# Two whole experts before the router, six after it; two attention units in flight; a new static order of steps

## The chip, the cores and the metric

The kernel runs on one core of a Trainium2 chip. The metric is the device time of the program in microseconds (us). The engines of the core are named as in the profile: PE (TensorE, the matrix engine; PEld is its weight load), DVE (VectorE), ACT (ScalarE), POOL (GpSimd) and SP (SyncE), which only issues DMAs here.

## What is computed

Attention with a decaying state, per batch (4) and head (8), over 768 tokens with a head size of 48; its output is read as 3072 tokens of 384 numbers, and a mixture of 8 experts follows. Every expert sees every token; the router only weighs the experts' outputs, and its weights need all tokens at once (the sums over axis 0).

```
state = alpha[t][:, None] * state + k[t] (x) v[t];   y[t] = q[t] @ state
x = y as [3072, 384]
P = exp(x @ w_gate - max);  8 times: P /= P.sum(1); P /= P.sum(0); P *= N / E
out = sum over e of P[:, e:e+1] * (relu(x @ w1[e]) @ w2[e])      # 384 -> 1024 -> 384
```

## The kernel before

**Two phases.** As the router's weights are known only when the last token is through the attention, the kernel computes whole experts early, beside the attention: for experts 0 to NA-1 (NA = 3) it stores the unweighted output of every token in DRAM (`raw`, evac_raw L275). The other experts come late, after the router (`sinkhorn` L998), and add weighted into `accd`. All matmuls of the experts are made of 16-bit halves, three passes each (PASSES).

**Early expert work** is cut into units of 256 tokens of one expert (moe_tile L236). A unit has 16 pieces: 8 of the first layer (9 matmuls of 256 columns each, tile `ps`, then ACT and DVE write the two halves of `h`) and 8 of the second (6 matmuls of 384 columns; after every fourth ACT copies the sum to `r`, which goes to `raw`). The list `waiting` (L910) opens a unit when its tokens and weights are there. `load_expert` (L157) loads and splits the weights of an early expert.

**Late expert work** goes by a scheme with seven products where eight blocks stand (first L1205, second L1407): per tile of 256 tokens 66 matmuls of 256 columns (`p1a`, `p1c`, `p1d`) and 84 of 192 (`p2x`, `p2y`, `p2v`). `load_late` (L1042) loads, splits and combines the weights of a late expert; for the first one, with w3_, that is done in the transition, beside the last early units, and for the others beside the expert ahead. The first two tiles of the first late expert have no partner yet: `first_one` (L1298) computes them in sixteen steps, and the loop at L1348 puts those between the last early pieces.

**Attention** goes by chunks of 128 tokens, 24 in all. The first four (direct_chunk L339) are computed from the inputs alone, in many small steps on PE and DVE. For the others a block of 256 tokens (attn_block L478, "b" steps) first works in a layout of 16 tokens per row: products on POOL (`tmp`), sums on DVE (`AB`), decays on both (`qt`, `kt`, `al`). There are ten such blocks, numbers 2 to 11. The block's results go to DRAM (`qs`, `ks`, `As`, `ds`) and come back in another layout (`QN`, `KN`, `an`, `DN`). Then attn_decays ("d") and, for each chunk, attn_chunk and attn_tail ("c", six steps): transposes into `Tk` and `Tq`, decayed copies (`deck`, `decq`), score matmuls (`psl`), the score tile `A` (POOL spreads `an` over it with `mask`), output (`psy`), state (`ST`), and at the end the chunk's router scores (`lg`, written by DVE from `psg`). All blocks use one set of buffers. turn_x (L770, "t") makes the combinations of x that the late experts need, on POOL.

**The order** of all steps of the early phase is the string ORDER (L40): b, w (weights), c, d, t, v (first weights of the late expert) and g (router weights) with the number of their block, expert or chunk; a capital letter moves a few operations from POOL to DVE or ACT. "f" is early expert work for 0.45 us of a time account (fill, L870). A step that may not run yet is put off (early_ L949, run L972). The engines then take their instructions in that program order, each engine in order, and wait for each other by semaphores. All DMAs are issued by SP, in order too.

## Time and profile before

| | |
|---|---|
| time, median of 3 runs | 1631.6 us (1631.49 to 1633.08) |
| the profiled execution, first to last instruction | 1630.9 us |
| PE busy | 1589.6 us (97%) |
| DVE busy | 1272.1 us (78%) |
| ACT busy | 932.6 us (57%) |
| POOL busy | 391.8 us (24%), all of it before 720 us |
| DMA | 188.5 MB, 39.8% of 16 engines |

How to read it: the profile is one execution. A busy share is an average over very different stages, so the table by stage, below, is the one to use. PE's spans are modelled, so that a busy PE need not do useful columns all the time. The chain of waits leads back from the last instruction to what released it at each step. A stage's idle time counts only on the engine that the others wait for.

The stages of the profiled execution: start (to 163 us, when the first chunk from a block has its scores), attention beside early experts (163 to 720), transition (720 to 797: the router's loop, the last early units and the first late steps) and the late experts (797 to 1625).

### The profile page before, as it was taken

The page shows a single profiled execution, that of the slowest core. Times are in us where ns is not written, and L with a number is a line of the kernel's source. Part 1 is how long each engine was busy: PE and PEld are TensorE (multiplying, and loading weights), DVE is VectorE, ACT ScalarE, POOL GpSimd, SP SyncE. Part 2 cuts the span into 40 slices and gives each one's busy share as a digit, 9 for nine tenths or more (in the row PEclk, how much of TensorE's full clock was granted, in tenths as well). Part 3 has the DMA queues.
Part 4 walks back from the last instruction along what each step waited for, and adds up shares of the span by engine and source line. Part 5 has one row for each costly group of instructions (what it writes and reads, how often), then busy time and mean ns, then how long its engine had stood idle before and what let it go on. Part 6 is the DMA issues. An engine that isn't in the chain of part 4 may idle for free.

```text
span 1630.9 us, 45380 instructions
## 1 busy us (share of the span) xinstructions
PE 1589.6 (97%) x18855; PEld 1370.0 (84%) x18855; DVE 1272.1 (78%) x2845; ACT 932.6 (57%) x2249; POOL 391.8 (24%) x402
## 2 busy tenths in 40 slices
PE   7799999999999999999999999999999999999999
PEld 5676777777777777777899999999999999999998
DVE  7978576755767655357879988998799879989997
ACT  4557443343343433435688877766776677665554
POOL 4526556845756743310000000000000000000000
PEclk9899999999999999999999999999999999999999
DMA  9262445154156143240433362326333532335443
GB/s 186 59 151 75 105 101 117 52 128 102 43 124 141 56 107 74 76 168 26 120 119 130 115 187 95 121 95 194 101 100 122 172 130 95 131 106 168 157 148 127
DMA packets 194654, 188.51 MB, mean 116 GB/s; under 512 B 115088, under 2 KB 175248, under 8 KB 194448
## 3 DMA queue, kind: packets, MB, share of 16 engines
q1 hardware_dynamic: 194448, 185.62, 39.8%
q8 instruction: 147, 2.41, 0.6%
q14 instruction: 59, 0.48, 0.1%
HBM read 129.76 MB, written 55.82 MB: 114 GB/s over the span
## 4 chain that ended last, share of the span: by engine, by line
PE 81%; DVE 11%; ACT 3%; issue 2%; DMA 1%; POOL 1%; SPq 0%; DVEq 0%; ACTq 0%; POOLq 0%
PE ps L66 30%; PE p1a L66 14%; PE p2x L66 12%; PE p2y L66 6%; PE p1c L66 4%; PE p1d L66 3%; PE p2v L66 3%; PE psl L66 2%; DVE h L57 2%; PE psy L66 2%; DVE hf L57 1%; DVE w L57 1%; DVE acc L57 1%; DVE AB L57 1%; PE pskn L69 1%
## 5 line engine op out<-in xcount | busy, mean ns | idle before, releaser
L66 PEld LDWEIGHTS <-h 128*128 128x128 f16 x6768 | 593.6, 98 | 119.8 <-issue 10.1
L66 PEld LDWEIGHTS <-w 128*128 128x128 f16 x4896 | 463.8, 98 | 64.3 <-issue 13.3
L57 DVE TENSOR_TENSOR h<-hf,h 128x256 f16<-128x256 f32 x480 | 286.3, 616 | 31.5 <-ACT h L57 31.0
L66 PE MATMUL ps<-xT,w 128*128 128x256 f16 (+1 forms) x2664 | 300.2, 270 | 4.1 <-DVE h L57 2.7
L66 PE MATMUL ps<-w,h 128*128 128x384 f16 x1728 | 298.5, 329 | 4.0 <-DVE w L57 2.9
L66 PE MATMUL p1a<-x,w 128*128 128x256 f16 (+1 forms) x1860 | 289.2, 269 | 4.4 <-ACT v L57 2.2
L66 PE MATMUL p2x<-w,h 128*128 128x192 f16 x2832 | 272.1, 246 | 0.0
L57 ACT CAST h<-hf 128x256 f16<-128x256 f32 x480 | 250.7, 571 | 14.8 <-DVE hf L57 10.8
L57 DVE TENSOR_TENSOR hf<-hf 128x256 f32<-128x256 f32 x480 | 182.1, 420 | 29.4 <-ACT hf L57 24.5
L66 PE MATMUL p1a<-x,wx 128*128 128x256 f16 (+1 forms) x744 | 199.6, 269 | 1.0 <-DVE p1c L57 1.0
L57 DVE SCALAR_TENSOR_TENSOR h<-ps,h 128x256 f16<-128x256 f32 (+1 forms) x296 | 115.7, 411 | 101.9 <-ACT h L57 100.7
L57 POOL TENSOR_TENSOR tmp<-qt,kt 128x768 f32<-128x768 f32 (+2 forms) x86 | 149.1, 1740 | 144.0 <-DMA kt<-in_k_dram 76.2
L57 ACT ACTIVATE h<-ps 128x256 f16<-128x256 f32 (+1 forms) x296 | 109.3, 376 | 129.7 <-PE ps L66 127.8
L66 PEld LDWEIGHTS <-wx 128*128 128x128 f16 x1736 | 167.3, 98 | 17.3
L57 ACT ACTIVATE hf<-p1d 128x256 f32<-128x256 f32 x120 | 46.0, 383 | 166.7 <-DVE h L57 140.9
L66 PE MATMUL p2y<-w,h 128*128 128x192 f16 x1416 | 136.1, 246 | 0.0
L57 ACT COPY r<-ps 128x384 f32<-128x384 f32 x72 | 34.3, 478 | 146.3 <-PE ps L66 112.5
L57 DVE TENSOR_REDUCE AB<-tmp 128x16 f32<-128x768 f32 (+2 forms) x90 | 81.1, 902 | 45.2 <-POOL tmp L57 44.3
L66 PE MATMUL p1c<-x,wx 128*128 128x256 f16 (+1 forms) x372 | 98.8, 269 | 0.0
L66 PE MATMUL p1d<-x,wx 128*128 128x256 f16 (+1 forms) x620 | 85.2, 269 | 0.0
L57 ACT COPY A<-psl 16x128 f32<-16x128 f32 (+3 forms) x148 | 49.2, 335 | 40.6 <-PE psl L66 39.1
L57 ACT ACTIVATE hf<-p1c 128x512 f32<-128x512 f32 x120 | 70.9, 591 | 0.0
(233 smaller groups left out, 1939.0 us busy)
## 6 DMA issues: line engine op xcount, KB each, us to landing
x<-xd SPq DMA_DIRECT2D x60, 704.0 KB, 5.4
accd<-acc SPq DMA_DIRECT2D x48, 384.0 KB, 3.2
acc<-accd SPq DMA_DIRECT2D x48, 384.0 KB, 3.2
raw<-r SPq DMA_DIRECT2D x72, 192.0 KB, 1.9
ri<-raw SPq DMA_DIRECT2D x72, 192.0 KB, 3.8
xT<-in_moe_w_dram SPq DMA_DIRECT2D x8, 768.0 KB, 5.5
w1f<-in_moe_w_dram SPq DMA_DIRECT2D x16, 384.0 KB, 7.4
w2f<-in_moe_w_dram SPq DMA_DIRECT2D x8, 768.0 KB, 6.6
```

Of the source, the lines that this page charges most:

```text
L57: r = f(*a, **k_)
L66: tc.keep_in_program_order(nc.tensor.matmul(out_, lhsT, rhs, start=start, stop=stop, **k_))
L69: tc.keep_in_program_order(nc.tensor.transpose(out=out_, in_=in_, identity=idn))
```

## The change

- NA goes from 3 to 2: experts 0 and 1 are early, 2 to 7 late. (A number TC allows the second early expert to take only the first tokens; it is set to all 3072.) The late list LATE has six experts. The raw outputs to be added are one with the first late expert and one with the last, where it was one and two.
- Blocks are computed on two sets of buffers in turn (`apx`, beside `ap1`), so that two are under way at once, except for blocks 2 and 3.
- A block's scores go to DRAM as 64 by 64 squares with zeros in place (`AS`, cleared twice by the new "z" steps), and come back with two DMAs per chunk straight into `A`. The POOL operation that made `A` out of `an` and `mask` is gone, and so are `an`, `mask`, and the clearing of `A` for each direct chunk. `ds` and `DN` are gone too: two matmuls with the identity give the decays (`psd`), and DVE copies them (`DT`), a 17th block step. `v` comes with one DMA per chunk where it was two.
- ORDER is new. "f" now is exactly one piece (piece). Conditions in early_ follow the new buffers.
- In the transition, w3_ starts only when one expert is left among the early units (before: when no unit of expert 0 was left), two turn steps move into the router's loop, and the first late tile gets eight steps between the last early pieces; the second tile's eight come after them. Tiles of late weights are renamed `lw`.

```diff
-    ORDER = 'D2 c6 C0 f f f f f f f f f f C0 f ...
-    NA = 3
+    ORDER = 'C0 C0 g C0 C0 B2 b2 b2 C0 B2 c1 w0 W0 g C0 B2 ...
+    NA = 2
+    TC = 3072
...
+    AA = [ap1.tile([P, H, P], F32, name=f"A{i}") for i in range(2)]
+    for x in AA:
+        GE.memset(x, 0.0)
+    AS = [dr.tile([H, NCH, P // BK, BK * BK + BK], F32, tag=f"As{i}", bufs=1, name=f"As{i}") for i in range(2)]
+
+    def clear_scores():
+        for x in AS:
+            SP.dma_start(x.rearrange("h c i a -> (h c i a)").rearrange("(p n t) -> p n t", n=5, t=208),
+                         AB[1].rearrange("p s t -> p (s t)")[:, :208].unsqueeze(1).to_broadcast([P, 5, 208]))
+            yield
...
     def load_v(x, b, t0):
-        for r in range(2):
-            SP.dma_start(x[:, :, r * DP:r * DP + D], v[b].rearrange("(j r) t d -> r t j d", r=2)[r, t0:t0 + P])
+        SP.dma_start(x.rearrange("p j (r e) -> p (j r) e", r=2)[:, :, :D], v[b, :, t0:t0 + P].rearrange("h t d -> t h d"))
...
-        qt, kt, al = (ap1.tile([P, 16, D], F32, tag=x, name=f"{x}_{nm}") for x in ("qt", "kt", "al"))
+        home = twin[0] if g > ND // NCH + 1 and g % 2 == 0 else ap1
+        qt, kt, al = (home.tile([P, 16, D], F32, tag=x, name=f"{x}_{nm}") for x in ("qt", "kt", "al"))
...
-        put(0, U)
-        dma(ds.rearrange("h n d -> n h d"), al[:, 0])
-        if True:
-            dma(As.rearrange("h (n s) t -> n h (s t)", s=16), Af)
+        psd = psa.tile([P, 512], F32, tag="psa", name=f"psd_{nm}")
+        for r in range(2):
+            mm(psd[r * DP:r * DP + D, :P], al[:, 0], ident)
+        for x, y in ((ks, ko), (qs, qo)):
+            dma(x.rearrange("h (n t) d -> (h n) (t d)", t=16), y.rearrange("p t d -> p (t d)"))
+        As_ = As[0]
+        dma(bass.AP(tensor=As_.tensor, offset=As_.offset, ap=[[16 * BK + 16, P], [BK, 16], [1, 16]]), A)
...
-        A = ap2.tile([P, H, P], F32, tag="A", name=f"A_{nm}")
-        GE.tensor_mul(A.rearrange("p h (n t) -> p n h t", t=16),
-                             got["an"][:, c].unsqueeze(1).to_broadcast([P, 8, H, 16]),
-                             mask.unsqueeze(2).unsqueeze(3).to_broadcast([P, 8, H, 16]))
+        A = AA[tt % 2]
+        for i in range(P // BK):
+            tok = slice(i * BK, (i + 1) * BK)
+            SP.dma_start(A[tok, :, tok], got["As"][:, c, i, :BK * BK].rearrange("h (s t) -> s h t", s=BK))
...
+    def piece():
+        if filler and (filler[0][2] != FT or filler[0][0] in ready):
+            x = filler[0]
+            next(x[1])
+            x[2] += 1
+            if x[2] == FT + 4 * (x[4] // P):
+                filler.pop(0)
...
-            while any(x[0] == 0 for x in filler):
-                yield 9.0
...
-    todo = [(e, t0) for e in range(NA, E) for t0 in range(0, NT, G)]
+    todo = [(e, t0) for e in LATE for t0 in range(start(e), NT, G)]
...
-        if n > 3:
+        if n == 2 or n == 3:
+            turn()
+        if n > 3 and len({x[0] for x in filler}) < 2:
             some(w3_, 0.45)
...
-            n = next(lead, None)
+            n = next(lead, None) if not filler or len(led) < 8 else None
...
-    RAWS = {NA: (0,), E - 1: (1, 2)}
+    RAWS = lambda e, t0: (0,) if e == NA else (NA - 1,) if e == E - 1 and t0 < TC else ()
```

How the change moves instructions is shown at three places. First, DVE around the score write of chunk 4, the first chunk that comes from a block (`lg` with `psg_0_4`). `h1` rows are evacuations of early first-layer pieces, `w21` rows weights of the last early expert. Before:

```order
L57 SCALAR_TENSOR_TENSOR w21_2_2265<-xT0_2_84,s_w2_2_2495,w20_2_2264 128x768 x2
L57 COPY p2t_89<-psg_0_4_2547 128x1
L57 TENSOR_SCALAR lg_88<-psg_0_4_2547,p2t_89,ipwg_93 128x8
L57 TENSOR_TENSOR Tq_0_5_2463<-Tq_0_5_2463,q128_0_2_1844 128x512
L57 SCALAR_TENSOR_TENSOR h1_2_0_2626<-ps1_2_0_0_2627,h0_2_0_2625 128x256
```

And now:

```order
L58 SCALAR_TENSOR_TENSOR h1_1_0_2213<-ps1_1_0_5_2320,h0_1_0_2212 128x256
L58 COPY p2t_85<-psg_0_4_2332 128x1
L58 TENSOR_SCALAR lg_84<-psg_0_4_2332,p2t_85,ipwg_89 128x8
L58 SCALAR_TENSOR_TENSOR w21_1_2131<-xT1_2_83,s_w2_1_2210,w20_1_2130 128x768
L58 TENSOR_SCALAR wsc_86<-p_w1_1_1474,p_w2_1_2207 128x1
```

Ahead of that write, PE has 216 first-layer matmuls of 256 columns, 144 of 128 and 192 of the second layer before, and 126, 144 and 96 now. On DVE 40 evacuations and 17 weight operations stand ahead of it before, 30 and 12 now.

Second, POOL at a chunk's decayed copy (`deck64`), in batch 2. Before:

```order
L57 TENSOR_TENSOR tmp1_2_2_55_6416<-qt_2_2_6107,kt_2_2_6108 128x384
L57 TENSOR_TENSOR deck64_2_2_6438<-Tk_2_2_6423,suf_1_137 128x256
L57 TENSOR_TENSOR A_2_2_6440<-an_2_1_6091,mask_71 128x8x8x16
L57 TENSOR_TENSOR kt_2_2_6108<-kt_2_2_6108,al_2_2_6109 128x8x48
L57 TENSOR_TENSOR tmp2_2_2_56_6459<-qt_2_2_6107,kt_2_2_6108 128x384
```

And now:

```order
L58 TENSOR_TENSOR tmp4_2_1_52_4669<-qt_2_1_3693,kt_2_1_3694 128x768
L58 TENSOR_TENSOR deck64_2_0_4710<-Tk_2_0_4695,suf_0_133 128x256
L58 TENSOR_TENSOR tmp4_2_2_53_4740<-qt_2_2_4662,kt_2_2_4663 128x768
L58 TENSOR_TENSOR tmp4_2_1_54_4742<-qt_2_1_3693,kt_2_1_3694 128x768
L58 TENSOR_TENSOR Tk_2_0_4695<-Tk_2_0_4695,k128_2_0_4646 128x512
```

The operation on `A` is gone, and products of two blocks (2_1 and 2_2) alternate where those of one block stood.

Third, DVE in the transition, at the second tile of the first late expert (`p1d_3_256` before, `p1d_2_256` now; `hf`, `h` and `p1c` belong to it too). Before:

```order
L57 SCALAR_TENSOR_TENSOR h1_2_2816_11673<-ps1_2_2816_7_11903,h0_2_2816_11672 128x256
L57 TENSOR_TENSOR xT1_0_85<-xT1_0_85,xT0_0_82 128x2x192
L57 TENSOR_TENSOR p1d_3_256_0_11878<-p1a_3_256_0_11876,v1_3_256_0_11896 128x256
L57 TENSOR_TENSOR h1_0_1_11582<-hf_3_0_1_11843,h0_0_1_11580 128x512 x2
L57 SCALAR_TENSOR_TENSOR w21_3_0_11116<-xT0_0_82,s_w2_3_11399,w20_3_0_11114 128x384
```

And now:

```order
L58 TENSOR_TENSOR hf_2_0_1_9868<-hf_2_0_1_9868 128x256 x4
L58 TENSOR_TENSOR p1d_2_256_0_9910<-p1a_2_256_0_9908,v1_2_256_0_9928 128x256
L58 TENSOR_TENSOR h_0_1_9628<-hf_2_0_1_9868,h_0_1_9628 128x512 x2
L58 TENSOR_TENSOR p1c_2_256_0_9909<-p1a_2_256_0_9908,v1_2_256_0_9928 128x256
L58 TENSOR_TENSOR h_0_1_9628<-hf_2_0_1_9868,h_0_1_9628 128x512
```

The last evacuation of an early first-layer piece stands right ahead of that tile before; now it stands one whole tile earlier, and the rest of the late weights (`lw21`) come after the tile. On PE, 36 second-layer matmuls of the last early unit stand between the second tile's steps before, and none now.

## Rows read from the trace of the kernel before

**Rows 1.** Busy time by stage (us, then number of instructions; clock, DMA share, GB/s).
```profile
core 0: us, PE busy (x) PEld busy (x) DVE busy (x) ACT busy (x) POOL busy (x), PEclk, DMA share, GB/s
0.00:25.00 25.00, 15.37 (x306) 12.65 (x307) 14.02 (x43) 6.87 (x14) 11.87 (x43) 1.00 0.93 162
25.00:85.00 60.00, 48.67 (x997) 38.79 (x994) 55.28 (x137) 34.02 (x72) 30.06 (x33) 0.86 0.47 113
85.00:163.00 78.00, 73.02 (x957) 55.34 (x955) 63.84 (x137) 49.14 (x112) 38.40 (x29) 0.98 0.43 106
163.00:720.00 557.00, 551.80 (x7144) 424.81 (x7142) 338.74 (x688) 225.63 (x621) 311.49 (x298) 1.00 0.40 96
720.00:797.00 77.00, 75.24 (x696) 58.14 (x695) 62.28 (x163) 41.84 (x96) 0.00 (x0) 1.00 0.18 65
797.00:1625.00 828.00, 823.69 (x8759) 778.83 (x8758) 735.76 (x1675) 575.07 (x1337) 0.00 (x0) 1.00 0.41 133
```

**Rows 2.** Chain that ended last, in order of time: start us, us, what.
```profile
748.08 15.68 PE ps L66 x120
...
1045.34 1.28 DVE w1f L57
...
1213.52 1.28 DVE w1f L57
...
1381.34 1.28 DVE w1f L57
```

**Rows 3.** Timeline of DVE at the scores of chunk 4 and the last chunk.
```profile
162.64 0.29 DVE L57 TENSOR_SCALAR lg<-psg,p2t,ipwg 128x8 f32<-128x8 f32 x1
...
706.27 0.28 DVE L57 TENSOR_SCALAR lg<-psg,p2t,ipwg 128x8 f32<-128x8 f32 x1
```

**Rows 4.** Groups of instructions, 0 to 163 us, PE: busy, mean ns, idle before.
```profile
L66 PE MATMUL ps<-w,h 128*128 128x384 f16 x192 | 36.3, 348 | 2.9 <-DVE w L57 2.9
L66 PE MATMUL ps<-xT,w 128*128 128x256 f16 (+1 forms) x365 | 35.2, 251 | 3.9 <-DVE h L57 2.4 <-DVE xT L57 1.3
```

**Rows 5.** Timeline at 674 us: POOL and DVE at one chunk's decayed copies.
```profile
675.04 2.08 POOL L57 TENSOR_TENSOR A<-an,mask 128x1024 f32<-128x1024 f32 x1
675.29 2.11 DVE L57 TENSOR_TENSOR deck<-Tk,k 128x256 f32<-128x256 f32 x1
677.33 0.65 DVE L57 TENSOR_TENSOR decq<-Tq,pre 128x256 f32<-128x256 f32 x1
```

**Rows 6.** Tiles deck and decq: min/median/max ns, first and last start.
```profile
L57 DVE TENSOR_TENSOR deck<-Tk,k x20: 673/2111/2115, 114.4 to 675.3; 128x256 f32<-128x256 f32 x20
...
L57 DVE TENSOR_TENSOR decq<-Tq,pre x20: 411/1210/2115, 116.5 to 677.3; 128x256 f32<-128x256 f32 x20
```

**Rows 7.** Groups of instructions, 163 to 720 us, POOL and DVE.
```profile
L57 POOL TENSOR_TENSOR A<-an,mask 128x1024 f32<-128x1024 f32 x18 | 36.8, 2047 | 0.0
...
L57 DVE SCALAR_TENSOR_TENSOR h<-ps,h 128x256 f16<-128x256 f32 x228 | 91.0, 418 | 88.7 <-ACT h L57 87.7
```

**Rows 8.** Waits, 165 to 720 us: us in total, times, longest.
```profile
POOL tmp L57 <- DMA kt<-in_k_dram: 70.6, 7, 20.7
...
DVE AB L57 <- POOL tmp L57: 42.0, 30, 3.4
```

**Rows 9.** Timeline of DVE in the transition, at the second late tile.
```profile
788.31 0.42 DVE L57 TENSOR_TENSOR p1c<-p1a,v 128x256 f32<-128x256 f32 x1
788.64 0.68 DVE L57 TENSOR_TENSOR h<-hf,h 128x512 f16<-128x512 f32 x1
...
790.63 0.61 DVE L57 SCALAR_TENSOR_TENSOR w<-xT,s_w,w 128x384 f16<-128x384 f32 x1
791.16 1.55 DVE L57 TENSOR_TENSOR hf<-hf 128x256 f32<-128x256 f32 x4
792.63 1.02 DVE L57 TENSOR_TENSOR xT<-xT 128x384 f32<-128x384 f32 x2
793.57 0.42 DVE L57 TENSOR_TENSOR p1d<-p1a,v 128x256 f32<-128x256 f32 x1
```

**Rows 10.** DMA issues: KB each, median us from issue to landing.
```profile
ks<-kt SPq DMA_DIRECT2D x10, 384.0 KB, 3.4
...
KN<-ks SPq DMA_DIRECT2D x20, 192.0 KB, 3.5
```

More of the change, by code (lines that the diff above doesn't have):

```diff
@@ L164, in load_expert @@
                 src = [(slice(0, P), w[e].rearrange("(c p) f -> p c f", p=P))]
-            hl = [(wpa[0] if e == NA - 1 else wp).tile([P, C, W], F16, tag=f"{nm}{i}", name=f"{nm}{i}_{e}")
-                  for i in range(2)]
-            res.append(hl)
-            hl = [x.rearrange("p c w -> p (c w)") for x in hl]
             r = 1 if nm == "w1" else 2
@@ L189, in load_expert @@
             cut = [slice(i * n, (i + 1) * n) for i in range(4)]
-            todo.append((nm, target, hl, cut, a))
+            todo.append((nm, target, C, W, cut, a))
             yield
-        for nm, target, hl, cut, a in todo:
+        for nm, target, C, W, cut, a in todo:
+            hl = [wp.tile([P, C, W], F16, tag=f"{nm}{i}", name=f"{nm}{i}_{e}")
+                  for i in range(2)]
+            res.append(hl)
+            hl = [x.rearrange("p c w -> p (c w)") for x in hl]
             ss = sm.tile([P, 4], F32, tag="wm", name=f"{nm}m_{e}")
@@ L581, in attn_decays @@
         nm = f"{b}_{u}"
[L582 to L588 removed]
+        dT = got["dT"]
         g2 = (b * NU + u) % 2
@@ L895, in tile_gla_moe @@
     wAB = [[] for _ in range(NA)]
-    w0, w1_, w2_ = (load_expert(e, wAB[e]) for e in range(NA))
+    wload = [load_expert(e, wAB[e]) for e in range(NA)]
     wgf = cp.tile([P, KT_, E], F32, name="wgf")
     gate = work_gate(wgf)
+    clear = clear_scores()
+    cleared = [0]
     hold[0] = True
@@ L909, in tile_gla_moe @@
     NS = 8
-    waiting = [(0, 0, 0, P), (0, 1, P, P), (1, 1, 0, U), (0, 3, U, U), (1, 3, U, U), (2, 1, 0, U), (2, 3, U, U)]
-    waiting += [(e, g * NCH + 1, g * U, U) for g in range(ND // NCH, len(units)) for e in range(NA)]
+    waiting = [(0, 0, 0, P), (0, 1, P, P), (1, 1, 0, U), (0, 3, U, U), (1, 3, U, U)]
+    waiting += [(e, g * NCH + 1, g * U, U) for g in range(ND // NCH, len(units)) for e in range(NA) if not e or g * U < TC]
     def act(a):
@@ L920, in act @@
         elif a == "f":
-            fill(0.45)
+            piece()
         elif a[0] == "b":
@@ L939, in act @@
             steps[n] += 1
-            if not wpa and min(steps[:ND]) > 12:
+            if not twin and min(steps[:ND]) > 12:
                 fst.close()
-                wpa.append(early.enter_context(tc.tile_pool(name="wpa", bufs=1, side="right")))
+                twin.append(at.enter_context(tc.tile_pool(name="apx", bufs=1)))
         for x in waiting[:]:
@@ L984, in tile_gla_moe @@
     while order:
+        n = len(order)
         order = run(order)
+        assert len(order) < n
     lop[0] = False
@@ L1026, in sinkhorn @@
         VE.tensor_mul(PR, PR, p2t.unsqueeze(2).to_broadcast([P, NTT, E]))
+    LATE = list(range(NA, E)) + [NA - 1] * (TC < NT)
+    start = lambda e: 0 if e >= NA else TC
     wl = {}
@@ L1345, in tile_gla_moe, with first_two @@
         bits(psva, x)
-    lead = iter((0, 0, 0, 1) + (2, 2, 1, 1) * 3)
+    def first_two():
+        for g in order_[:2]:
+            yield from first_one(g, xq[0])
+    lead, led = iter((0, 0, 0, 1) + (2, 2, 1, 1) * 3), []
     F = None
     while filler or F is None:
-        some(w3_, 0.9 if F is None else 0.62)
+        if len({x[0] for x in filler}) < 2:
+            some(w3_, 0.9 if F is None else 0.62)
         if NA in ready1 and (not filler or left() < LEAD):
             if F is None:
-                F = chain(*(first_one(g, xq[0]) for g in order_[:2]))
-            n = next(lead, None)
+                F = first_two()
+            n = next(lead, None) if not filler or len(led) < 8 else None
             if n is not None:
+                led.append(n)
                 next(F)
@@ L1387, in fetch_raws @@
             home = hpa.tile([P, 8, 2, P], F32, tag="hf", bufs=1, name="ri").rearrange("p n j t -> p (n j t)")
-        for k_, i in enumerate(RAWS.get(e, ())):
+        for k_, i in enumerate(RAWS(e, t0)):
             for z in range(2):
@@ L1519, in tile_gla_moe @@
                 next(new, None)
-                if now == 2 and order_[n + 1][0] > NA:
+                if now == 2 and order_[n + 1][0] != NA:
                     fetch_raws(*order_[n + 1])
```

142 lines of the change are left out of this document (71 added, 71 removed).

## The prediction

> **What bounds the kernel now.** I read the table by stage first [rows 1]. Before 25 us no engine is full. From 25 to 85 us DVE works 55.28 of 60 us and PE 48.67: DVE sets the pace. From 85 us on PE is the bound: idle 5.0 us to 163 us, 5.2 us in the attention stage, 1.8 us in the transition and 4.3 us in the late stage. So time falls where PE loses work or where the start gets shorter, and it rises where PE runs dry. The chain that ended last [rows 2] agrees: an early unit of 120 matmuls on PE, then one late expert after another.
>
> The profiled execution spans 1630.9 us, the median of the runs is 1631.6; I sum against the span and add 0.7 at the end. A measurement can tell about 0.2% from no change, 3.3 us here.
>
> **One expert moves from early to late.** An early unit is 72 matmuls of 256 columns and 48 of 384, 36,864 columns, and takes 15.68 us [rows 2]; twelve units are 188.2 us. That is 0.425 ns a column: 0.109 us for 256 columns, 0.163 us for 384. A late expert takes the distance between two `w1f` on the chain: 1213.52 - 1045.34 = 168.2 and 1381.34 - 1213.52 = 167.8 us, with its weights and its adding of products. Gain: 188.2 - 168.0 = **20.2 us**. The columns agree: 66 x 256 + 84 x 192 = 33,024 a tile, 0.896 of before. This is all the gain that the change has on PE.
>
> **The start.** The router needs the last chunk, the chunks pass through one chain, and the first chunk from a block has its score at 162.64 us [rows 3]. PE work that stood ahead of this score and now stands behind it is no longer cover for the start: 90 matmuls of 256 columns and 96 of 384 (from the two orders; before they are part of [rows 4]), 90 x 0.109 + 96 x 0.163 = 25.5 us. If the score keeps its time, 25.5 us come back later; if it comes earlier, that much less. So the question is when it comes. DVE works 14.02 + 55.28 + 63.84 = 133.1 us to 163 us [rows 1]. The change takes ten evacuations of 418 ns [rows 7] and five weight operations of about 1.2 us (half as wide is 0.61 us [rows 9]) off it, 10.2 us, and adds some 6 us of small products, sums and copies that move from POOL or come with the second block: 129 us. From 25 us on, 115 us are left. If DVE is kept as full as between 25 and 85 us (92%), the score comes at 25 + 115/0.92 = 150 us; full, at 140; at the mean of 25 to 163 us, 119.1/138 = 86%, at 158 us. PE then loses 12.9, 2.9 and 20.9 us. I take 93.5%, near the row of the stretch where DVE does set the pace: 148 us, and a **loss of 10.5 us**.
>
> **The attention stage.** PE must not run dry between 148 us and the last score. The room between a chunk's six steps is nearly the same in the two orders: in pieces of early work, the medians are 9, 6.5, 3.5, 6 and 9 before and 10.5, 6, 3, 4.5 and 9.5 now. A block's steps now spread over 52 to 66 pieces, where 30 to 55 were, as two are under way. That covers POOL's longest wait now, seven times and up to 20.7 us for the block's own loads, since one set of buffers must come free first [rows 8]; DVE's 30 waits for POOL's products, 42 us, get room likewise. From the write of `ks` to the first transposes stand 4 to 18 pieces (0.98 us each, 15.68/16), 6 at the least favourable later block, 5.9 us; write and read back last 3.4 and 3.5 us [rows 10], so one or two chunks may wait 1 to 2 us each, less what PE has ahead. The `A` squares come by DMA beside them, and have until the output, three steps later.
>
> DVE and POOL get denser. Work is the same, time is one expert shorter: 551.8 - 188.2 + 25.5 of PE work, less what the score's time left behind, is about 384 us. DVE: 338.7 us, less 80 evacuations of expert 2 (33.4 us) and 7 us of its weights, is 298 us, 78% of 384 against 61% before. But one thing is relieved. Beside POOL's `A` of 2.08 us, DVE's `deck` lasts 2.11 us and ends when `A` ends [rows 5], and its median over 20 is 2.11 us with a minimum of 0.67; `decq`, 1.21 against 0.41 [rows 6]. With `A` gone, deck may be 0.67 again, or be held by `tmp` instead: up to 1.4 us in each of 18 chunks; I take 1.3, 23 us. DVE is then at 275 us, 72%. POOL loses the 36.8 us [rows 7]: 275 us of 384, 72% against 56%. Two engines at 72%, with room by the order, hold PE: I take **0**, range -2 (of the 5.2 us idle) to +14.
>
> What rows 5 show is in the Trainium skill a rule: the page "SBUF — State Buffer", Terms, has DVE and GpSimd share one port pair, "Lock-allocated, exclusive, held for the full instruction". The trace agrees, in that deck ends with `A`. The rule cuts both ways: it makes the removed `A` worth more than POOL's time, and it makes two engines at 72% each, whose operations with two operands exclude one another, more than either can hold. The second is the slower rival below.
>
> **The transition.** After the last score, 4 early units and a piece are left in both orders. Two things change. The second late tile's eight steps stand without early matmuls between them: 36 second-layer matmuls (36 x 0.163 = 5.9 us) stood there before, as cover. In that stretch DVE has some 15 us to do, in the form of [rows 9] (four `hf` 1.55, two `xT` 1.02, `h` 0.68, `p1c` and `p1d` 0.42, weights 0.61), and PE 9.2 us; the difference, 5.9 us, is what PE waits if DVE has it all in that stretch. The 5.9 us of early work are not gone, but run earlier. And the first late expert's second-layer weights start with two units (31.4 us) of PE work left, not three (47 us); before, though, the router's loop took DVE's first part of that. I take +5 us, from 0 (DVE has done part of it ahead) to +10 (weights late too).
>
> **The end.** The last late expert adds one raw output instead of two: DVE work and DMAs beside a PE that is busy 823.7 of 828 us [rows 1], so 0. Fewer DMAs on SP (some 45 of 675) free a queue on which nothing waits in the rows above: 0.
>
> **Sum.** 1630.9 - 20.2 + 10.5 + 0 + 5 = 1626.2 us; with 0.7, **1627 us**.
>
> **Rivals.**
> Floor: DVE is full from 25 us on, so the score comes at 140 us (+2.9), the transition costs nothing, and 2 us of idle go: 1631.6 - 20.2 + 2.9 - 2 = 1612.3 us. For it: `A`, which also ran beside DVE in the start, is gone, and steps of two blocks fill gaps. Against: 92% is the most that any stage shows.
> No difference: the terms are at their poorer ends, 86% to 92% in the start, +13 to +17, and 8 us in the transition: 1631.6 - 20.2 + 13 + 8 = 1632.4 us, and somewhat to either side. For it: every term except the first is a cost, and they add to what the expert brings.
> Slower: DVE and POOL do not keep up in the attention stage. Without the relief DVE needs 298 us; if POOL's denser operations hold it so that it gets no more than 75% of the time, the stage takes 298/0.75 = 397 us where PE has 384, and with the waits of a chain of steps in order a few us more: +17, at 1627 + 17 = 1644 us. At 72% it is 414, +30 and 1657 us. It decides from the point where the share that DVE needs is more than it gets: 78% without relief, 72% with it. For it: `deck` at 2.11 where 0.67 is enough shows how much POOL can hold DVE [rows 6], and POOL goes from 56% to 72%. Against: in the start DVE had 92% beside POOL at 30.06 of 60 us [rows 1].
> That the change doesn't do what it says is no rival: the two orders show the units, the missing `A` and the second set of buffers.
>
> **How the numbers follow.** The forecast, 1620 to 1628, 34%; the floor and what lies between it and 1620, 12%; no difference, 1628.3 to 1634.9, 24%; slower, 30%. Faster by over 0.2% (below 1628.3) is 46%, slower (above 1634.9) 30%. The range goes from the floor less 1 us, 1611, to 1649, above the 75% case and below the 72% one, and leaves out some 2 in 10, mostly above.
>
> **What would show it.** In the profile of the changed kernel: the score of chunk 4 at 148 us (140 to 158); PE idle by at most 5 us from there to the last score; that last score near 530 us, where it stood at 706 [rows 3]; `deck` at a median of 0.7 to 0.9 us; POOL waiting for its loads for less than 20 of the 70.6 us; about 5 us of PE idle at the second late tile; late experts 168 us apart. PE idle in many small pieces between 148 and 530 us, behind DVE or POOL, is the slower rival; behind `KN` or `QN`, it is the round trip; a late score of chunk 4 with DVE under 90% is the start. What would make me wrong altogether is a late expert that takes other than 168 us, since six of them now stand where five did.

## The result: slower by 0.6%, where 0.3% faster was forecast

The changed kernel takes 1642.2 us (median; 1641.0 to 1644.2), the kernel before 1632.3 us in the same runs. The ratio is 1.0059, with a 95% interval of 1.0045 to 1.0073. The forecast was 1627 us; its range, 1611 to 1649, holds the time, but its direction is wrong.

The profiled execution spans 1640.0 us, against 1630.9 before. Its stages, with the boundaries where they now stand (us and number of instructions for each engine; then granted clock, DMA share, GB/s), answer to [rows 1]:

```profile
core 0: us, PE busy (x) PEld busy (x) DVE busy (x) ACT busy (x) POOL busy (x), PEclk, DMA share, GB/s
25.00:85.00 60.00, 45.37 (x915) 38.02 (x911) 52.81 (x140) 27.38 (x59) 21.14 (x25) 0.94 0.55 138
85.00:149.60 64.60, 61.83 (x1023) 48.01 (x1021) 56.74 (x131) 40.56 (x98) 32.56 (x29) 0.98 0.40 107
149.60:538.80 389.20, 380.70 (x5745) 291.51 (x5746) 295.47 (x602) 172.91 (x493) 250.45 (x261) 1.00 0.47 121
538.80:641.30 102.50, 87.35 (x776) 67.06 (x774) 68.21 (x178) 48.80 (x113) 5.00 (x10) 0.96 0.36 115
641.30:1634.00 992.70, 989.65 (x10505) 935.47 (x10505) 873.10 (x1987) 690.56 (x1604) 0.00 (x0) 1.00 0.38 124
```

In the fourth of these lines, the transition, PE is idle for 15 of 102.5 us. In the like stretch before, from just behind the last score to the first full late step, it is idle for 3.5 of 94.4 us:

```profile
706.50:800.90 94.40, 90.94 (x817) 69.54 (x816) 68.57 (x182) 48.99 (x115) 2.35 (x4) 1.00 0.23 80
```

No other stage after the start has such a gap. In the attention stage PE is idle for 8.5 us (5.2 before).

Three landmarks divide the span: the scores of chunk 4 and of the last chunk, which answer to [rows 3], and the end. DVE's timeline of the changed kernel has the first two:

```profile
149.34 0.28 DVE L58 TENSOR_SCALAR lg<-psg,p2t,ipwg 128x8 f32<-128x8 f32 x1
...
538.49 0.28 DVE L58 TENSOR_SCALAR lg<-psg,p2t,ipwg 128x8 f32<-128x8 f32 x1
```

Early expert work falls by 188.2 us of PE in all. Counted in the two orders by columns, 25.5 of it fall ahead of chunk 4's score, 155.8 between the two scores and 6.9 behind the last one; one more late expert adds 167.9. What each part took beyond that:

| part | before | after | difference | expert work there | the rest | forecast |
|---|---|---|---|---|---|---|
| to chunk 4's score | 162.6 | 149.3 | -13.3 | -25.5 | **+12.2** | +10.5 |
| from there to the last score | 543.6 | 389.2 | -154.5 | -155.8 | **+1.3** | 0 |
| from the last score to the end | 924.6 | 1101.5 | +176.9 | +161.0 | **+15.9** | +5 |
| sum | 1630.9 | 1640.0 | +9.1 | -20.3 | +29.4 | +15.5 |

The column of early work goes by the order of the instructions. At chunk 4's score PE had already done 3.9 us of early work that stands behind this score in the order (144 and 108 matmuls of 256 and 384 columns, where 126 and 96 stand ahead of it). Counted by what was done, the first two rows would be +8.7 and +5.4. So the border between them is not sharp; the third row, +15.4 in that count, hardly depends on it.

So 11 of the 14 us that the forecast missed lie behind the last score. The late experts are not the reason: they follow each other at 1390.82 - 1222.99 = 167.83 us (DVE's timeline; before 167.8 to 168.2, [rows 2]).

```profile
1222.99 1.28 DVE L58 SCALAR_TENSOR_TENSOR lw1f<-lw1f,s_w,lwx 128x1024 f32<-128x1024 f32 x1
...
1390.82 1.28 DVE L58 SCALAR_TENSOR_TENSOR lw1f<-lw1f,s_w,lwx 128x1024 f32<-128x1024 f32 x1
```

The chain that ended last shows the place (start, us, what; changed kernel):

```profile
577.68 0.49 ACT r L58
...
578.19 0.32 SPq L58
...
578.56 4.62 DMA xT<-in_moe_w_dram
...
587.69 0.09 ACT w2b L58
587.78 0.04 issue
587.82 0.16 PE pst_w L67
587.99 18.08 PE ps L67 x120
```

`xT<-in_moe_w_dram` is the load of the first late expert's second-layer weights. It goes out 40.1 us after the last score. The rows ahead of it show what it waited for at the end: SP issues in order, and ahead of the load stood the store of an early output (`r`), which waited for ACT. In the timeline of the kernel before it goes out at 717.21, 10.9 us after:

```profile
717.21 1.58 SPq L57 DMA_DIRECT2D xT<-in_moe_w_dram  x2
```

ACT makes sums of squares (`w2b`) from it, and PE reduces them in a single small matmul (`pst_w`). PE works in order, so the early pieces queued behind that matmul wait too: 5.58 us, in PE's timeline. The 120 matmuls behind it are an early unit; they take 18.08 us where the like unit took 15.68 [rows 2]. The granted clock of that stretch is 0.87 on average: right after the idle time PE ran at the lower level, 1.2 GHz (0.50), until about 593 us, and from 594 us at 2.4 GHz again (windows of the changed kernel):

```profile
575.00:588.00 13.00, 7.42 (x61) 5.79 (x60) 2.77 (x8) 5.43 (x15) 0.00 (x0) 0.92 0.42 137
588.00:606.10 18.10, 18.10 (x124) 13.04 (x123) 12.68 (x26) 10.42 (x19) 0.00 (x0) 0.87 0.07 23
588.00:592.00 4.00, 4.00 (x20) 2.86 (x19) 1.16 (x7) 0.50 (x2) 0.00 (x0) 0.50 0.02 4
592.00:594.00 2.00, 2.00 (x14) 1.39 (x13) 0.61 (x2) 0.88 (x3) 0.00 (x0) 0.80 0.00 0
594.00:606.10 12.10, 12.10 (x94) 8.79 (x92) 10.91 (x18) 9.05 (x16) 0.00 (x0) 1.00 0.09 33
```

At the end of the transition PE waits once more, 5.04 us, for ACT's `v`, which stands in ACT's queue behind its splitting of those weights:

```profile
587.82 0.16 PE L67 MATMUL pst_w<-w2b,onesb 128*128 128x4 bf16 x1 [5.58 <-ACT w2b L58]
...
641.30 0.80 PE L67 MATMUL p1a<-x,lw 128*128 128x256 f16 x3 [5.04 <-ACT v L58]
```

Of the signs that the forecast named, three came out or nearly so: the score of chunk 4 at 149.3 us (148), late experts 168 us apart, and `deck` at a median of 0.64 us (0.7 to 0.9), where it was 2.11 [rows 6]. Four did not. The last score stands at 538.5 us (near 530). PE is idle for 8.5 us between the two scores (at most 5), 6.0 of them in four waits for DVE. POOL's wait for its loads fell from 70.6 [rows 8] to 30.6 us (under 20). PE idles for 8.2 us from 606 to 641 us, around the second late tile (about 5). The row of the tile `deck` (min/median/max ns) and that of PE's waits in the attention stage (us, times, longest):

```profile
L58 DVE TENSOR_TENSOR deck<-Tk,k x20: 411/644/1376, 104.7 to 518.2; 128x256 f32<-128x256 f32 x20
```

```profile
PE ps L67 <- DVE h L58: 6.0, 4, 3.0
```

### The profile page after: what moved, and what is told of

Read it like the earlier page. It is cut to its first block, busy times and chain, and to the rows that moved or that the text cites. A ratio compares the mean times of both kernels' runs of the same rounds, so it can differ in the third digit from the quotient of the medians.

```text
span 1640.0 us, 46289 instructions
## 1 busy us (share of the span) xinstructions
PE 1579.3 (96%) x19189; PEld 1392.1 (85%) x19189; DVE 1363.1 (83%) x3071; ACT 985.3 (60%) x2376; POOL 321.5 (20%) x361
## 4 chain that ended last, share of the span: by engine, by line
PE 78%; DVE 12%; ACT 3%; issue 2%; POOL 2%; DMA 2%; SPq 1%; ACTq 0%; DVEq 0%; POOLq 0%
PE p1a L67 18%; PE ps L67 17%; PE p2x L67 15%; PE p2y L67 8%; PE p1c L67 5%; PE p1d L67 4%; PE p2v L67 4%; PE psl L67 2%; DVE h L58 2%; PE psy L67 2%; DVE hf L58 1%; SPq L58 1%; DVE acc L58 1%; POOL tmp L58 1%; DVE AB L58 1%
## 5 line engine op out<-in xcount | busy, mean ns | idle before, releaser
L58 DVE TENSOR_TENSOR h<-hf,h 128x256 f16<-128x256 f32 (+1 forms) x576 | 344.4, 617 | 35.4 <-ACT h L58 34.8
L67 PE MATMUL p1a<-x,lw 128*128 128x256 f16 (+1 forms) x2220 | 347.1, 270 | 9.3 <-ACT v L58 7.5
L67 PE MATMUL p2x<-lw,h 128*128 128x192 f16 x3408 | 327.6, 246 | 0.9 <-DVE p2y L58 0.9
L58 ACT CAST h<-hf 128x256 f16<-128x256 f32 (+1 forms) x576 | 300.6, 571 | 17.0 <-DVE hf L58 12.3
L67 PEld LDWEIGHTS <-lw 128*128 128x128 f16 x2664 | 253.1, 98 | 35.2 <-issue 13.1
L67 PE MATMUL p1a<-x,lwx 128*128 128x256 f16 (+1 forms) x888 | 239.0, 270 | 1.0 <-DVE p1c L58 1.0
L67 PEld LDWEIGHTS <-lwx 128*128 128x128 f16 x2072 | 200.2, 98 | 21.0
L67 PEld LDWEIGHTS <-w 128*128 128x128 f16 x1800 | 171.2, 100 | 33.5 <-issue 10.4
L67 PE MATMUL p2y<-lw,h 128*128 128x192 f16 x1704 | 163.8, 246 | 0.0
L67 PE MATMUL p1c<-x,lwx 128*128 128x256 f16 (+1 forms) x444 | 118.7, 270 | 0.0
```

Of the source, the lines that this page charges most:

```text
L58: r = f(*a, **k_)
L67: tc.keep_in_program_order(nc.tensor.matmul(out_, lhsT, rhs, start=start, stop=stop, **k_))
```

## The experiments

Times are medians. All runs have the kernel before beside them (1632.3 to 1633.8 us), and comparisons between runs go by the ratio to it (the changed kernel: 1.0059).

### The transition: load, cover, and the start of the splitting

**e1_early_load** puts back the early load; the tile `w1h`, which takes expert 0's room, is asked for after the scales and not ahead of the load.

```diff
-        w1h = [wp.tile([P, 6, HW], F16, tag=f"w1{i}", name=f"lw1{i}_{e}") for i in range(2)]
+        if e != NA:
+            w1h = [wp.tile([P, 6, HW], F16, tag=f"w1{i}", name=f"lw1{i}_{e}") for i in range(2)]
...
+            while len({x[0] for x in filler}) > 1:
+                yield 9.0
+            w1h = [wp.tile([P, 6, HW], F16, tag=f"w1{i}", name=f"lw1{i}_{e}") for i in range(2)]
...
-        if n > 3 and len({x[0] for x in filler}) < 2:
+        if n > 3:
             some(w3_, 0.45)
...
-        if len({x[0] for x in filler}) < 2:
-            some(w3_, 0.9 if F is None else 0.62)
+        some(w3_, 0.9 if F is None else 0.62)
```

> The changed kernel with one thing put back: the load of the first late expert's second-layer weights, and the sum of squares that its scale is made from, may run in the router's loop, while units of both early experts are left. Only the splitting of the weights, which needs the room of expert 0's weights, still waits until one expert is left. Theory (the transition was mis-sized, because the load is now issued some 40 us after the last score, 578.6 against 538.5, and PE waits in order for the sum made from it): the wait of 5.6 us before the one-matmul sum goes, the 120 matmuls behind it take 15.7 us again and not 18.1, together 8.0 us; and as the splitting starts at once when one expert is left, some of the 5.0 us that PE waits after the second late tile goes too. 1642.2 - 8 = 1634, down to 1629. Rival (the lost time comes from the start and the attention stage, and PE would only wait later for the router or for the weights): 1640 to 1643, with the idle time of PE standing a few us further on.

**e2_second_tile** gives the second late tile its cover back; half of its `h` goes to spare rows of tiles of the first late tile.

```diff
...
+            a = [wp.tile([P, 11, 2, P], F16, tag=f"w2{i}", name=f"h{i}_0_0") for i in range(2)]
+            t = wx.tile([P, 3, 7, 2, P], F16, tag="wx", name="h_0_1")
+            rows2.extend((t[:, 2], a[0][:, 7:10], a[1][:, 7:11]))
...
-            n = next(lead, None) if not filler or len(led) < 8 else None
+            n = next(lead, None) if len(led) < 12 or all(x[2] >= FT for x in filler) else None
```

> The changed kernel, but the second late tile's eight steps stand between the last early pieces again, as before the change; its halves find room in spare parts of other tiles. Nothing else is moved; the load of the second-layer weights is as late as in the changed kernel. Theory (cover): PE idles 8.2 us from 606 to 641 us in the changed kernel, 2.8 us in the like stretch before; the difference, 5.4 us, goes: 1636 to 1638. Rival (DVE's splitting of the late weights sets the end of this stretch, whatever PE has for cover): no change, 1641 to 1643.

**e3_both** has the two edits together.

> Both edits in one: the early load and the second late tile between the last early pieces. Theory (the transition lost 16 us against the sum, some 13.5 of it by these two): 1642.2 - 8.0 - 5.4 = 1629, and PE idle from the last score to the first full late step under 5 us. Rival (the two waits are one and the same wait for the weights, and either edit alone takes it away): no more than the better of the two alone.

Measured: e1 1641.5 us (1.0050), e2 1646.3 (1.0080), e3 1641.2 (1.0054). None of the three gave what its theory expected (1629 to 1634, 1636 to 1638 and 1629 us). e2 came out a little slower than its rival, but not in the transition: from the last score to the end it takes 1101.6 us where the changed kernel takes 1101.5, as the rival had it. In e1 the wait at `pst_w` is gone, but the wait at the end of the transition grew from 5.04 to 8.03 us (PE's timeline), and the first split of the weights on DVE starts only 51.8 us after the last score (544.29):

```profile
642.73 0.80 PE L67 MATMUL p1a<-x,lw 128*128 128x256 f16 x3 [8.03 <-ACT v L58]
```

```profile
596.13 0.75 DVE L58 SCALAR_TENSOR_TENSOR lw<-xT,s_w,lw 128x512 f16<-128x512 f32 x1 [4.24 <-ACT lw L58]
```

So the two waits of PE are signs, and not the cause: take one away and the other grows. From the last score to the end e1 takes 1097.8 us, 3.7 less than the changed kernel, where 8 to 13 were expected. Cover for the second tile is worth nothing as long as this is so: e2 against the changed kernel, and e3 (1097.7 us) against e1, differ by 0.1 us in that stretch. That pointed at the splitting itself. In e1 the room for the split weights was still asked for late: the rule waits for one expert to be left, and is looked at in coarse steps (`yield 9.0`).

**e5_gate_first_layer** lets the splitting go when the room is really free, that is, when expert 0's last unit is through its first layer.

```diff
+            while any(x[0] == 0 and x[2] < FT for x in filler):
+                yield 0.45
```

(in place of the two lines of e1; the rest as e1)

> The changed kernel with the early load of the run e1_early_load, and with the splitting of the first late expert's weights let go as soon as the last unit of expert 0 is through its first layer (it takes the place of expert 0's first-layer weights alone), looked at after every step. What is computed is the same. Theory, formed on e1 to e3 (the length of the transition is set by DVE and ACT splitting these weights: from the first split to the first full late step 51.4 us before the change and 46.9 after it, whether PE has cover or not; so what counts is how long after the last score the first split starts: 43.2 us before, 55.9 in the changed kernel, 51.8 in e1): the first split starts some 30 to 40 us after the last score, and the stretch from the last score to the first full late step falls from 102.8 to 88 to 92 us, where PE's own work ends: 1642.2 less 11 to 15 is 1627 to 1631. Rival (DVE has the router's loop to do at that time and the split only fills the gaps, so an earlier start makes it longer): 97 to 100 us, 1637 to 1640.

**e6_gate_and_tile** adds e2's edit to it.

> The run e5_gate_first_layer and in it the second late tile's eight steps between the last early pieces, as in e2_second_tile. Theory (the weights start in time, so that PE's cover counts now, and the waits of 0.4 to 1.2 us within the second tile's steps go): 2 to 5 us less than e5_gate_first_layer. Rival (cover counts for nothing, as in e2): the same as e5_gate_first_layer within 1.5 us.

**b2_late_gate** goes the other way: the kernel before with the changed kernel's rule, and nothing else.

```diff
-        if n > 3:
+        if n > 3 and len({x[0] for x in filler}) < 2:
             some(w3_, 0.45)
...
-        some(w3_, 0.9 if F is None else 0.62)
+        if len({x[0] for x in filler}) < 2:
+            some(w3_, 0.9 if F is None else 0.62)
```

> The kernel before with the changed kernel's rule for the first late expert's second-layer weights alone: nothing of them, the load too, until one expert is left among the early units (two units, 31.4 us of PE work, in both kernels); the rest as before. Theory (the rule is the change's loss in the transition): the load is issued some 40 us after the last score and not 11, the first split starts some 55 us after it and not 43, and the time rises by 8 to 13 us: 1640 to 1645. Rival (the loss in the transition comes from the order of the last early steps, the two moved turns or the second tile): 1631 to 1634.

Measured: e5 1631.4 us (0.9987, interval 0.9972 to 1.0003), e6 1629.0 (0.9965, 0.9952 to 0.9977), b2 1651.8 (1.0113, 1.0096 to 1.0130). By the ratios e5 gives back 12 us, e6 15, and the rule alone costs the kernel before 18, more than its theory had (8 to 13). e5 is not told apart from the kernel before; e6 is faster than both kernels. In the timelines, from the last score to DVE's first split, from there to PE's first matmul of a late second layer (`p2x`), and from the last score to the end of the profiled execution:

| | last score | first split | after (us) | first p2x | split to p2x (us) | score to p2x (us) | score to end (us) |
|---|---|---|---|---|---|---|---|
| before | 706.3 | 749.5 | 43.2 | 802.1 | 52.6 | 95.8 | 924.6 |
| after | 538.5 | 594.4 | 55.9 | 643.6 | 49.2 | 105.1 | 1101.5 |
| e1 | 544.3 | 596.1 | 51.8 | 645.0 | 48.9 | 100.7 | 1097.8 |
| e2 | 542.8 | 598.9 | 56.2 | 647.3 | 48.3 | 104.5 | 1101.6 |
| e3 | 539.0 | 590.8 | 51.8 | 639.7 | 48.9 | 100.7 | 1097.7 |
| e5 | 544.3 | 584.3 | 40.0 | 637.3 | 53.0 | 93.0 | 1088.5 |
| e6 | 538.3 | 578.3 | 40.0 | 628.8 | 50.5 | 90.5 | 1085.9 |
| b2 | 710.9 | 773.6 | 62.6 | 823.1 | 49.5 | 112.2 | 942.7 |

In all eight rows the column "split to p2x" is 48 to 53 us: two kernels, with and without cover, with and without the wait at `pst_w`. Where the splitting starts late (after, e1, e2, e3, b2) it is 48.3 to 49.5 us, whatever cover PE has; DVE is busy 41.4 of these 49.2 us in the changed kernel, and PE 41.0. Where it starts early (before, e5, e6) it is 50.5 to 53.0, and PE's own work fills more of it (49.9 of 52.6 us in the kernel before). So with a late start, the length of the transition is the start of the splitting plus about 49 us for the steps on DVE and ACT; with an early one, PE's own work comes near to setting it. In the last column e5 gives back 13.0 us and e6 15.6, all but 0.3 of the 15.9 us that the transition cost, and b2 adds 18.0 to the kernel before. The rows behind the table for the kernel before, the changed kernel, e5 and b2:

```profile
749.45 0.75 DVE L57 SCALAR_TENSOR_TENSOR w<-xT,s_w,w 128x512 f16<-128x512 f32 x1
```

```profile
594.42 0.75 DVE L58 SCALAR_TENSOR_TENSOR lw<-xT,s_w,lw 128x512 f16<-128x512 f32 x1 [0.19 <-ACT lw L58]
```

```profile
584.33 0.75 DVE L58 SCALAR_TENSOR_TENSOR lw<-xT,s_w,lw 128x512 f16<-128x512 f32 x1 [1.74 <-ACT lw L58]
```

```profile
773.58 0.75 DVE L57 SCALAR_TENSOR_TENSOR w<-xT,s_w,w 128x512 f16<-128x512 f32 x1 [0.19 <-ACT w L57]
```

Only where the splitting starts early does the cover of the second tile count: e6 takes 2.4 us less than e5 (2.6 in the last column), as its theory had it, and in the transition of e6 PE works 84.3 of 88.8 us:

```profile
538.60:627.40 88.80, 84.30 (x776) 65.60 (x774) 67.55 (x178) 47.42 (x112) 5.02 (x10) 1.00 0.26 89
```

### The start

**e4_start_less** takes eight pieces of early work out of the order of the steps ahead of chunk 4's score, one in about every fifth place, and puts them one by one behind it, over the whole attention stage (`f` in ORDER moved, nothing else).

> The changed kernel with eight early pieces (54 matmuls of 256 columns and 12 of 384, 18,432 columns, 7.8 us of PE at 0.425 ns a column) taken out of the steps ahead of the score of chunk 4 and spread over the steps behind it. All other steps keep their order. Theory (DVE paces the start, 92% busy): six evacuations of 0.42 us less on DVE bring the score only some 2.7 us forward, 149.3 to 146.6, and the time rises by 7.8 - 2.7 = 5 us to 1647. Rival (PE paces the steps ahead of this score): the score comes 7.8 us earlier and the time stays at 1642. Other rival (the chunk's own chain of small steps or the loads pace it): the score stays near 149 and the time rises by 7.8 us to 1650.

**e8_start_block** takes the same eight out, and puts them in one row right behind that score:

(only the place behind the score is shown)

```diff
-... w1 f C4 w1 t f f f c5 ...
+... w1 f C4 f f f f f f f f w1 t f f f c5 ...
```

> The eight early pieces that e4_start_less took out of the start, taken out again, but put in one row right behind the score of chunk 4, so that from there on every step meets the same pieces of early work as in the changed kernel. Theory (DVE paces the start, and e4 rose by 28 us because its eight pieces, half a unit, made the first-layer pieces, with their evacuations on DVE, meet other steps of the attention through most of the stage): the score near 146, the last score 3 to 6 us later than 538.5, 1645 to 1649. Rival (the attention stage has no room for later work, whatever its place): 1660 or more, as e4.

Measured: e4 1670.8 us (1.0244), e8 1652.0 (1.0113); both are above what their theories had, 1647 and 1645 to 1649. The score of chunk 4 stands at 145.95 and 147.09 in these, 3.4 and 2.2 us earlier than in the changed kernel. But six profiles with the same code up to there (the changed kernel, e1, e2, e3, e5, e6) have it at 146.2 to 151.5, 149.0 in the mean, so that a step of 2 to 3 us is hardly told from none. One of 7.8 us would show: PE's early pieces do not pace the start. What does is seen only in its last part. The router matmuls of chunk 4 start on PE at 142.6 to 146.8 us in the six profiles, at 143.2 in e4 and at 144.2 in e8, no earlier than the others. The score follows them by 3.6 to 4.8 us in the six, by 2.8 and 2.9 in e4 and e8: DVE's queue ahead of the score got shorter by about 2 us, as six evacuations (2.5 us) let expect. In the changed kernel DVE works without a break from 135.7 us to the score, which waits there behind the splitting of two weights. So DVE sets the last few us of the start. Whether it sets the rest too, or the chunk's own chain of small steps does, is not told apart. The rows of PE, for the changed kernel and e8:

```profile
144.59 0.37 PE L67 MATMUL psg<-wg,xT 128*128 128x8 f16 x9
```

```profile
144.23 0.37 PE L67 MATMUL psg<-wg,xT 128*128 128x8 f16 x9
```

What the pieces cost behind the score is another matter. e8 adds 7.8 us of work there and the stage from score to score takes 400.1 us, 10.9 more (8 more than the mean of the six profiles, 392.2). e4 adds the same work and takes 421.2 us, 32 more. PE is idle in it for 10 us of the first 104, where the changed kernel has 1 of 96 (e4, windows):

```profile
146.20:250.00 103.80, 94.03 (x1260) 71.24 (x1259) 78.69 (x150) 39.90 (x121) 65.48 (x65) 0.95 0.46 122
250.00:350.00 100.00, 92.05 (x1412) 69.40 (x1409) 77.13 (x150) 40.41 (x115) 60.39 (x62) 0.98 0.49 127
```

Half of a unit's pieces need DVE (first layer), half don't. e4 moves this pattern by up to half a unit against the attention's steps, and e8 moves it back at once. That this makes the 19 us between the two runs is a reading that no run here shows, and which of the steps pays is not told apart.

### The attention stage

**e7_pool_op** gives POOL an operation as long as the one that the change removed.

```diff
...
+        GE.tensor_mul(junk_[0], junk_[0], junk_[1])
         A = AA[tt % 2]
```

> The changed kernel with one operation of POOL added in each of the 20 chunks that come from blocks, at the place where the spreading of A stood: a product of 128x1024 numbers of a spare tile by itself, 2.05 us each. Nothing reads it. Theory (the forecast's: an operation of two operands of DVE beside it ends with it, and the attention stage has room for that): deck back to about 2.1 us, DVE some 20 us busier from 150 to 540 us, and the last score 0 to 6 us later: 1642 to 1648. Rival (DVE is so full in the first 100 us of that stage, 85 of 96 us, that every us it is held shows): the last score 15 to 30 us later, 1657 to 1672.

**e10_pool_fill** keeps POOL nearly as long, but reads nothing (the edit against e7):

```diff
-        GE.tensor_mul(junk_[0], junk_[0], junk_[1])
+        [GE.memset(junk_[0], 0.0) for _ in range(2)]
         A = AA[tt % 2]
```

> As e7_pool_op (1667.0 us, last score 23.7 us later than in the changed kernel), but in place of the product of 2.05 us that reads a tile, POOL fills the spare tile twice with zeros, about 0.95 us each, which reads nothing. Theory (it is the hold on DVE that costs: e7's deck has a median of 1.74 us where the changed kernel has 0.64): deck stays near 0.65 us and most of the 25 us goes away, 1642 to 1650. Rival (POOL's own queue is what sets the pace, at 250 of 389 us busy, and two us more a chunk show whatever the operation reads): 1660 to 1667.

**b1_no_spread** takes POOL's spreading of `A` out of the kernel before; it leaves out that part of the attention.

```diff
...
-        A = ap2.tile([P, H, P], F32, tag="A", name=f"A_{nm}")
-        GE.tensor_mul(A.rearrange("p h (n t) -> p n h t", t=16),
-                             got["an"][:, c].unsqueeze(1).to_broadcast([P, 8, H, 16]),
-                             mask.unsqueeze(2).unsqueeze(3).to_broadcast([P, 8, H, 16]))
+        A = AA[tt % 2]
```

> The kernel before, without POOL's spreading of an over A in the 20 chunks from blocks, and without the clearing of A in the four direct ones: the score tiles' diagonal parts stay zero, so this part of the attention is left out. Theory (in the kernel before PE bounds the attention stage, with DVE at 61%, so that POOL's operation costs nothing there, though it holds deck): deck falls to about 0.67 us, DVE gets 20 us of idle time more, and the time stays within 4 us, 1628 to 1632; so what e7 shows is a price of the denser order, not of the operation as such. Rival (POOL's operation cost as much before as in e7): 1607 to 1615.

Measured: e7 1667.0 us (1.0210), e10 1650.6 (1.0107), b1 1631.4 (0.9986, interval 0.9976 to 0.9995). So e7 came out as its rival, with the last score 23.7 us later; e10 just above its theory's range, and b1 within it. The tile `deck` in e7, e10 and b1 (min/median/max ns):

```profile
L58 DVE TENSOR_TENSOR deck<-Tk,k x20: 411/1740/2112, 103.1 to 541.9; 128x256 f32<-128x256 f32 x20
```

```profile
L58 DVE TENSOR_TENSOR deck<-Tk,k x20: 409/415/1230, 103.0 to 522.7; 128x256 f32<-128x256 f32 x20
```

```profile
L57 DVE TENSOR_TENSOR deck<-Tk,k x20: 410/700/1372, 116.7 to 675.5; 128x256 f32<-128x256 f32 x20
```

The stage from score to score in e7 and e10 (windows):

```profile
152.30:562.40 410.10, 385.40 (x5745) 293.29 (x5746) 317.19 (x602) 172.85 (x493) 287.20 (x279) 0.98 0.45 115
```

```profile
147.90:543.30 395.40, 381.22 (x5745) 291.35 (x5746) 284.70 (x601) 173.96 (x493) 281.12 (x297) 1.00 0.46 119
```

Some 2 us of POOL per chunk (medians of 2.07 in e7, twice 0.95 in e10) cost 25 us if the operation reads a tile and 8 if it only writes. With the reading operation DVE is busy 317.2 us in that stage, with the writing one 284.7 (295.5 in the changed kernel). So some 16 of the 25 us go with reading, and what goes with reading is the hold on DVE. The other 8 come although DVE has less to do than in the changed kernel; POOL's own queue is the likely cause, which no run here shows. The spreads of the two runs, 1665.7 to 1670.4 and 1646.3 to 1653.5, don't touch. In the kernel before the operation cost 2 us and no more, though it held `deck` there even longer (2.11 us): PE was busy for all but 5.2 us of that stage, and DVE for 61% of it. Removing it was worth nearly nothing in the old order; in the new one its return costs 25 us.

The rule of the Trainium skill for this is on the page "SBUF — State Buffer", section "Who interferes with whom": a DVE instruction with two SBUF inputs contends with a GpSimd instruction that reads SBUF, not with one that only writes it. The two medians of `deck`, 1.74 and 0.42 us, agree.

**e9_one_set** puts all blocks on one set of buffers.

```diff
-        home = twin[0] if g > ND // NCH + 1 and g % 2 == 0 else ap1
+        home = ap1
...
-            return (done[m] == 15 and not past(m - 2) or done[m - (1 if m < one + 2 else 2)] < 17
+            return (done[m] == 15 and not past(m - 2) or done[m - 1] < 17
```

> The changed kernel with all blocks on one set of buffers (qt, kt, al and the products) as before the change; a block's steps are put off until the block ahead has done its last. The rest of the order, and all that is computed, stays. Theory (with one expert less the attention stage is paced by DVE and POOL, and the second set is what keeps them fed): POOL waits for its loads 50 to 80 us in that stage where it is some 30 in the changed kernel, and the last score comes 15 to 40 us later, 1657 to 1682. Rival (the two sets are not needed; room in the order is enough): 1640 to 1648.

Measured: 1829.0 us (1.1197), far beyond its theory. POOL waits 121.2 us for its loads (waits of POOL, 150 to 720 us), and the last score stands at 726.7 us, 188 later than in the changed kernel, where 15 to 40 were expected. But this order was written for two sets; an order made for a single set, with one expert less early, was not run. The run shows that this order hangs on the second set, not what the set is worth by itself.

```profile
POOL tmp L58 <- DMA kt<-in_k_dram: 121.2, 7, 21.5
```

## Why the prediction was wrong, step by step

- **One expert from early to late: right.** 168.0 us forecast for the late expert, 167.8 measured.
- **The start: near in size, in part by luck.** 148 us forecast for the score, 149.3 measured; 12.2 us lost, not 10.5. The forecast had 115 us of DVE work from 25 us on, at a share of 93.5%. Measured are 109.3 us at 88%, little more than the 86% before; under 90% was the forecast's own sign that the start is the weak place. The two errors cancel: 115 us at 88% would give 156 us, 109.3 at 93.5% would give 142. That PE's early pieces do not set the score is shown (e4, e8); that DVE does is shown for its last few us only.
- **The attention stage: right within its range, with two engines loaded otherwise than forecast.** 0 was forecast, with a range of -2 to +14; +1.3 measured. The changed kernel's profile is the shortest of the six with the same code (389.2 to 395.4 us from score to score, 392.2 in the mean), so +4 is the better number. The slower rival, that DVE and POOL cannot hold the pace, did not decide, but shows in small: PE's 8.5 us of idle time are mostly waits for DVE. e7 shows how near it was: with a like operation back on POOL the rival comes true, at 25 us. The sum had DVE at 275 us and POOL at 275; measured are 295.5 (76%) and 250.5. The relief of 23 us came (`deck` and the `decq` made with `pre` fell from 49.6 to 26.0 us in this stage). But the new order lets DVE do seven of the large products (`tmp`, 15.0 us) where it did three (5.2), and the 7 us of weights that the sum took off are in no row of that stage before. The last score came at 538.5 and not near 530: 6.9 us of early work moved ahead of it, which I had counted as equal on both sides ("4 early units and a piece are left in both orders" holds at the end of the order's list, not at the last score).
- **The transition: the step that failed.** I gave the second tile's missing cover 5.9 us, and the later weights next to nothing, since "the router's loop took DVE's first part of that" before, and took +5 in all, with +10 (weights late too) as the bad end. It cost 15.9. So the late weights were named, and priced far too low. The cover was worth nothing by itself (e2) and 2.6 us once the weights were early (e6); the late weights cost nearly all: e5 mends their start alone, to a little earlier than before (40.0 us after the last score, 43.2 before), and gives back 13.0 us of this stage, and b2 puts the late start into the kernel before and costs 18. The mistake was to price the step by the engine's busy time (DVE was taken by the router) and PE's cover left (31.4 us for 47), and not by its chain: the load's issue, its landing (4.62 us), four sums of squares on ACT, PE's reduction, five small operations on DVE, and only then a split of about 50 us. Before the change all but the last stood under the router's loop; the new condition in the code puts the load, too, behind it. In the trace of before, the load at 717.21 and the first split at 749.45, right at the loop's end, were there to be read. The diff moved one condition from the splitting (`while any(...)` after the scales) to the whole of `w3_`, and I followed the splitting alone.
- **The rivals and the range.** The rival of no difference had the transition at 8 us and the start at +13; the case that came true has the start near that (12.2) and lies beyond it in the transition alone (15.9). The time, 1642 us, is near the 1644 of the slower rival, for another reason. That the range, which was drawn up to 1649 for that rival, holds the time is luck.

With the load and the splitting mended (e5) the kernel takes 1631.4 us, 2.4 less than before in the same runs, which the interval does not tell from no difference. With the second tile's cover too (e6) it takes 4.8 less; the forecast's step from before to after was 4.6.

## What to carry to other kernels

When a condition is put on a whole sequence of steps, price the sequence from its first DMA to its last consumer, and look in the trace for the work under which its front half lay until now. A wait that the trace names can be a symptom: in e1 it went away and another grew by 3 us, and only the table of one nearly fixed length (split to `p2x`) over several runs showed what set the end. An operation on an engine that is not the bound can be nearly free in one order (2 us, b1) and cost 25 us in a denser one (e7).

## What was not expected of the hardware

POOL filling a tile (e10) left DVE's decayed copy of two operands, `deck`, at a median of 0.42 us, less than beside POOL's usual products (0.64 us in the changed kernel), while a product on POOL in the same place (e7) held it at 1.74. And one idle gap of PE cost more than its 5.6 us: the 120 matmuls behind it took 18.08 us where they took 15.68 before, with the granted clock at 0.50 for the first 4 us and at 0.87 in the mean (1.00 from 588 to 606 us in e5, where there is no such gap).
